# A gate as a VectorE dot product, W loaded by two queues, and w2 ahead of a shuffle

## Chip, cores and metric

One core of a Trainium2 chip. The metric is device time in microseconds (us) of one execution; medians are given with the range of all runs. Ratios are the mean time of one kernel's fast runs over that of the other's of the same rounds, with a 95% interval, so they are not quite the ratio of the medians quoted. The kernel before runs 144.71 us (144.64 to 145.56, three runs).

## The reference, cut to what matters

```python
x = A_x                                        # 2048 x 512 (and a batch of 1)
g = sigmoid((x * gate_w).sum(-1, keepdims=True))
a = irfft2(rfft2(x) * (w_r + 1j * w_i))        # spectral branch, W is 2048 x 257
h = x @ w1 + b1                                # dense branch, 512 -> 1792
b = (h * tanh(softplus(h))) @ w2               # 1792 -> 512
return g * a + (1 - g) * b
```

## The kernel before

Everything is in bf16 with float32 sums. The spectral branch is written as small DFT matmuls. It runs in stages: column transforms (s1) and row transforms (A1) of 16 row blocks, a shuffle through scratch in DRAM (four writes, four reads), the middle stage (s2, the products with W on VectorE, s2i), a second shuffle, and two inverse stages (s1i, a1i). The dense branch has 56 groups of four matmuls in layer 1 and 34 groups of seven in layer 2. Its groups fill TensorE wherever the spectral branch has nothing ready.

The order on each engine is fixed when the kernel is built. A scheduler in the kernel's own source lists the tasks by priority with planned durations; a transfer is planned at a bandwidth written beside it. The engines then run these lists in order and wait on semaphores.

```python
DMA_BW = 370e3          # planned bytes per us of a transfer
W_BW = 150e3            # the same, for the reversed rows of W
...
            if t.isdma:                                   # in schedule()
                xs = max(est + t.dur + 1.2, bw_free)
                bw_free = xs + t.xfer                     # one transfer after the other
                t.done = bw_free + 0.9
...
        def wload(nm, dst, src_t, o):                     # W: plain and reversed half
            v = src_t.rearrange("(g h e2 j) k -> g h e2 j k", g=16, h=2, e2=2)
            dma(f"ld_{nm}p", dst[0:32, :, :].rearrange("p j k -> p (j k)"), v[:, 0, ...]...,
                32 * 16448, writes=[(o, 0)])
            nb = dst[32:64, :, :]
            ...
            dma(f"ld_{nm}r", back(0, 31, 16, 32, 2), n1, 16 * 32 * 514, writes=[(o, 1)], bw=W_BW)
            dma(f"ld_{nm}n", back(1, 31, 16, 31, 2), n0, 16 * 31 * 514, writes=[(o, 2)], bw=W_BW)
            ...
        wload("wr", Wa, A_w_r, "Wa")
        wload("wi", Wb, A_w_i, "Wb")
        dma("ld_sm", SM[:], d_c["SM"][:], ...)            # matrices of the middle stage
        # W's upper partitions: four copies on VectorE, with a high priority
                G.add(f"cp{o}{h}", [("dve", ..., lambda e, ...: e.tensor_scalar(
                    out=W[64:128, js, :], in0=W[0:64, js, :], scalar1=sc, ...))],
                      reads=[(o, i) for i in range(4)], writes=[(o, 4, h)], prio=PR["cp"])
...
        for h in range(2):                                # w2 waits for the shuffle's writes
            dma(f"ld_w2_{h}", w2_sb[:, 7 * h:7 * (h + 1), :], ..., writes=[("w2", h)],
                deps=t_r1w, queue="pool")
        # the shuffle's reads overwrite x_sb; t_r1w are its writes
            t_r1r.append(dma(f"r1r{h}", In2[:, 8 * h:8 * h + 8, :]..., reads=[("scr1", i) for i in range(4)], ...))
...
        def f_gate(e):                                    # gate: 64 one-column matmuls
            for t in range(NT):
                for dt_ in range(4):
                    ins = e.matmul(ps[:, bk(sl_g), t:t + 1], xT[:, dt_, t, :], gw_sb[:, dt_:dt_ + 1], ...)
```

## Time and profile before

| | before |
|---|---|
| time, median | 144.71 us |
| last A1 matmul starts | 30.61 us |
| last write of the first shuffle landed, reads issued | 37.97 us |
| first s2 matmul | 42.0 us, after a wait of 0.8 |
| granted TensorE clock | 1.00 |

How to read it: TensorE is nearly always busy, so the time is its work plus its holes. The lines of the profile itself stand in the prediction.

### The profile page before, as it was taken

To read this page: it belongs to the slowest core of one execution; us is meant where nothing else is said; L and a number is where in the kernel's file an instruction comes from. 1 tells how busy PE (TensorE), PEld (TensorE's weight loads), DVE (VectorE), ACT (ScalarE), POOL (GpSimd) and SP (SyncE) were. 2 spreads that over 40 slices of the span, in tenths; PEclk is the share of its full clock that TensorE was granted. 3 is DMA by queue.
4 is the path that set the end of the run, shared out by engine and by line. 5 is a ranking of instruction groups with operands and counts; after the bars stand their busy time and mean duration, and the time that the engine had idled before them with its cause. 6 is when DMAs were issued, how large, how long until landed. Compare 5 with 4: busy or idle time off the path is not lost.

```text
span 142.7 us, 2376 instructions
## 1 busy us (share of the span) xinstructions
PE 134.9 (95%) x866; PEld 72.9 (51%) x881; DVE 86.1 (60%) x188; ACT 82.9 (58%) x139; POOL 3.9 (3%) x10
## 2 busy tenths in 40 slices
PE   6999999778979999999999999999999999999992
PEld 2476665554434444434444465455456565555471
DVE  2448694974009999999971031002999985899331
ACT  3289888776867877779984573855154344431000
POOL 1000000000160000000000000000000000000000
PEclk9999999999999999999999999999999999999999
DMA  4999999999299999580303695000012120100121
GB/s 117 302 405 408 249 172 151 150 307 336 74 310 359 364 317 145 131 283 0 147 0 152 174 292 121 0 0 5 0 74 76 74 76 5 74 0 36 43 108 39
DMA packets 20463, 21.66 MB, mean 152 GB/s; under 512 B 5156, under 2 KB 16932, under 8 KB 20388
## 3 DMA queue, kind: packets, MB, share of 16 engines
q1 hardware_dynamic: 19712, 18.89, 49.6%
q0 software_dynamic: 704, 2.62, 5.2%
q8 instruction: 7, 0.11, 0.3%
q14 instruction: 4, 0.03, 0.1%
q10 hardware_dynamic: 36, 0.00, 0.0%
HBM read 14.17 MB, written 6.29 MB: 143 GB/s over the span
## 4 chain that ended last, share of the span: by engine, by line
PE 70%; DVE 13%; DMA 7%; ACT 4%; issue 3%; DVEq 0%; SPq 0%
PE ps L824 28%; PE ps L804 21%; PE ps L885 5%; PE ps L530 4%; DMA scr<-R 4%; DVE PX L764 3%; DVE PX L760 3%; DVE PX L763 3%; DMA R<-scr 3%; PE ps L866 3%; PE ps L654 2%; ACT R L516 2%; DVE PX L767 2%; DVE R L515 1%; PE ps L779 1%
## 5 line engine op out<-in xcount | busy, mean ns | idle before, releaser
L824 PE MATMUL ps<-w_sb,hsb 128*128 128x512 bf16 (+1 forms) x232 | 51.3, 366 | 0.6 <-DMA w_sb<-in_B_w_dram 0.2
L804 PE MATMUL ps<-xT,w_sb 128*128 128x512 bf16 x215 | 51.3, 379 | 0.4
L812 ACT ACTIVATE hsb<-ps,b1f 128x512 bf16<-128x512 f32 x56 | 37.7, 689 | 11.1 <-PE ps L804 10.8
L516 ACT ACTIVATE R<-ps 128x512 bf16<-128x512 f32 (+1 forms) x43 | 24.7, 596 | 16.3 <-PE ps L824 11.2
L824 PEld LDWEIGHTS ps<-w_sb,hsb 128*128 128x128 bf16 x238 | 22.7, 98 | 22.4 <-DMA w_sb<-in_B_w_dram 0.5
L804 PEld LDWEIGHTS ps<-xT,w_sb 128*128 128x128 bf16 x224 | 21.2, 98 | 22.9 <-ACT xT L621 0.2
L516 ACT ACTIVATE PX<-ps 128x512 bf16<-128x512 f32 (+1 forms) x19 | 10.5, 551 | 6.8 <-PE ps L885 4.2
L515 DVE CAST R<-ps 128x512 bf16<-128x512 f32 (+1 forms) x17 | 11.3, 689 | 3.3 <-PE ps L654 1.6
L876 ACT ACTIVATE TT<-ps 128x512 bf16<-128x512 f32 x11 | 6.4, 595 | 6.5 <-PE ps L866 6.4
L897 DVE SCALAR_TENSOR_TENSOR PX<-ps,gcol,R 128x512 f32<-128x512 f32 x12 | 9.0, 751 | 1.4 <-DVE R L891 0.5
L873 DVE CAST TT<-ps 128x512 bf16<-128x512 f32 x5 | 3.4, 689 | 9.7 <-PE ps L866 8.9
L885 PE MATMUL ps<-GD,TT 128*128 128x256 bf16 x64 | 9.0, 273 | 0.0
L530 PE MATMUL ps<-GD 128*128 128x512 bf16 x18 | 7.3, 522 | 1.3 <-DVE GD L527 1.3
L885 PEld LDWEIGHTS ps<-GD,TT 128*128 128x128 bf16 x64 | 6.2, 98 | 3.3 <-DVE TT L873 0.3
L852 DVE TENSOR_SCALAR gcol<-gth 128x16 f32<-128x16 f32 x1 | 0.2, 174 | 12.3 <-ACT gth L849 12.3
L767 DVE TENSOR_TENSOR PX<-PX 128x512 bf16<-128x512 bf16 x16 | 6.8, 425 | 1.0
L763 DVE TENSOR_TENSOR PX<-PX,Wb 64x512 bf16<-64x512 bf16 x16 | 6.8, 422 | 0.5
L764 DVE TENSOR_TENSOR PX<-PX,Wb 64x512 bf16<-64x512 bf16 x16 | 6.7, 421 | 0.2
L760 DVE TENSOR_TENSOR PX<-PX,Wa 128x512 bf16<-128x512 bf16 x16 | 6.7, 421 | 0.1
L923 DVE SCALAR_TENSOR_TENSOR R<-ps,omg,R 128x512 bf16<-128x512 f32 (+1 forms) x5 | 3.2, 643 | 5.8 <-PE ps L824 5.8
L903 DVE SCALAR_TENSOR_TENSOR R<-ps,gcol,PX 128x256 bf16<-128x256 f32 x12 | 5.8, 484 | 0.4
L654 PEld LDWEIGHTS ps<-CF,R 128*128 128x128 bf16 x64 | 4.7, 101 | 2.6 <-issue 0.6
(93 smaller groups left out, 110.9 us busy)
## 6 DMA issues: line engine op xcount, KB each, us to landing
scr<-R SPq DMA_DIRECT2D x8, 512.0 KB, 4.6
R<-scr SPq DMA_DIRECT2D x8, 512.0 KB, 6.0
w_sb<-in_B_w_dram SPq DMA_DIRECT2D x2, 896.0 KB, 8.8
w_sb<-in_B_w_dram POOLq DMA_DIRECT2D x2, 896.0 KB, 11.4
out_dram<-R SPq DMA_DIRECT2D x7, 256.0 KB, 2.0
R<-in_A_x_dram SPq DMA_DIRECT2D x3, 512.0 KB, 11.3
SM<-c_sm SPq DMA_DIRECT2D x1, 576.0 KB, 10.9
Wa<-in_A_w_r_dram SPq DMA_DIRECT2D x1, 514.0 KB, 13.9
```

The costliest lines, as they stand in the source:

```text
L515: G.add(name, [("dve", dve_dur(n), lambda e: e.tensor_copy(out=outf(), in_=inf())), ("act", act_dur(n), lambda e: e.activation(outf(), inf ...
L516: ("act", act_dur(n), lambda e: e.activation(outf(), inf(), AF.Copy))],
L530: G.add(f"warm{i}", [("pe", 0.43 if i < 7 else 0.22, lambda e, sl=sl: e.matmul(ps[:, bk(sl), :], GDf[:, 0:128], GDf[:, 0:512], start=True, ...
L760: return e.tensor_tensor(out=v(P1, sP, 0, 128), in0=v(Xb, sX, 0, 128), in1=Wa[:, js, 0:256], op=ALU.mult)
L763: e.tensor_tensor(out=v(P2, sQ, 0, 64), in0=v(Xb, sX, 64, 128), in1=Wb[64:128, js, 0:256], op=ALU.mult)
L764: return e.tensor_tensor(out=v(P2, sQ, 64, 128), in0=v(Xb, sX, 0, 64), in1=Wb[0:64, js, 0:256], op=ALU.mult)
L767: return e.tensor_tensor(out=P1[:, sP.i, :], in0=P1[:, sP.i, :], in1=P2[:, sQ.i, :], op=ALU.add)
L804: ins = e.matmul(ps[:, bk(sl), :], w1_sb[:, dt_, 128 * ft:128 * (ft + 1)], xT[:, dt_, 4 * c:4 * c + 4, :], start=(dt_ == 0), stop=(dt_ == 3))
L812: return e.activation(hsb[:, hb, ft, :], ps[:, bk(sl), :], AF.Mish, bias=b1f[:, ft:ft + 1])
L824: ins = e.matmul(ps[:, bk(sl), 0:n1 - n0], hsb[:, hb, ft, 128 * tl:128 * (tl + 1)], w2_sb[:, ft, n0:n1], start=(ft == 0), stop=(ft == NFT ...
L885: ins = e.matmul(ps[:, bk(sy), 256 * hh:256 * (hh + 1)], TT[:, st.i, i, :], GD[:, i, :], start=(i % 2 == 0), stop=(i % 2 == 1))
L897: return e.scalar_tensor_tensor(out=o, in0=ps[:, bk(sy), 0:256].unsqueeze(1).to_broadcast([128, 2, 256]), scalar=gcol[:, t:t + 1], in1=ya[ ...
```

## The change

The intent is fourfold. The gate leaves TensorE: VectorE multiplies and sums x with gate_w in an idle stretch. The W copies go behind the last evacuation of the front, so that A1 waits less. W's reversed rows come by GpSimd's queue while the plain rows come by SP's. w2 is loaded ahead of the shuffle, so that layer 2 can start early. The planned bandwidths are changed with it. The diff, cut to its core (left out: reordered loads of x and w1 with planned bandwidths of their own, the smaller transpose without gate_w, planned durations of the warming matmuls, and a priority):

```diff
-DMA_BW = 370e3
+DMA_BW = 380e3
-W_BW = 150e3
+W_BW = 260e3
...
             dma(f"ld_{nm}p", dst[0:32, :, :]..., 
-                32 * 16448, writes=[(o, 0)])
+                32 * 16448, writes=[(o, 0)], bw=260e3)
...
-            dma(f"ld_{nm}r", back(0, 31, 16, 32, 2), n1, 16 * 32 * 514, writes=[(o, 1)], bw=W_BW)
+            dma(f"ld_{nm}r", back(0, 31, 16, 32, 2), n1, 16 * 32 * 514, writes=[(o, 1)], bw=W_BW, deps=t_wq, queue="pool")
   (the same for the other reversed rows)
...
         dma("ld_sm", SM[:], d_c["SM"][:], 128 * 2 * 128 * len(MATS), writes=["SM"])
-        (the four W copies stood here)
+        for h in range(2):
+            dma(f"ld_w2_{h}", w2_sb[:, 7 * h:7 * (h + 1), :], ..., 128 * 7 * 1024,
+                writes=[("w2", h)])
...
-        for h in range(2):
-            dma(f"ld_w2_{h}", ..., writes=[("w2", h)], deps=t_r1w, queue="pool")
...
+                G.add(f"cp{o}{h}", ..., reads=[(o, i) for i in range(4)], writes=[(o, 4, h)], deps=t_e2, prio=PR["cp"])
...
+            t_gx.append(G.add(f"gx{t}", [("dve", 0.8, lambda e, t=t: e.scalar_tensor_tensor(
+                out=gscr[:, t % 3, :], in0=x_sb[:, t, :], scalar=1.0, in1=gwb[:, :], op0=ALU.mult, op1=ALU.mult, accum_out=gacc[:, t:t + 1]))],
+                reads=[("x", t), "gwb"], writes=[("gacc", t), ("gscr", t % 3)], deps=t_e2, prio=PR["cp"] + 0.2))
...
-                reads=[("scr1", i) for i in range(4)], writes=[("In2", h)], deps=t_x1, prio=PR["ld"] + 1))
+                reads=[("scr1", i) for i in range(4)], writes=[("In2", h)], deps=t_x1 + t_gx[4 * h:4 * h + 4], prio=PR["ld"] + 1))
...
-        (f_gate and its 64 matmuls)
+        G.add("gth", [("act", 1.6, lambda e: e.activation(gth[:, :], gacc[:, :], AF.Tanh, scale=0.5))],
+              reads=[("gacc", t) for t in range(NT)], writes=["gth"], deps=t_hs, prio=PR["gate"])
```

More of the change, by code (lines that the diff above doesn't have):

```diff
@@ L433, in _build @@
         tz = sb("tz", [128, 2, 32], F32)
-        bgraw = sb("bgraw", [18, 128], BF)
+        bgraw = sb("bgraw", [NFT, 128], BF)
         b1f = sb("b1f", [128, NFT], F32)
-        gw_sb = sb("gw_sb", [128, 4], BF)
+        gwb = sb("gwb", [128, 512], BF)
+        gacc = sb("gacc", [128, NT], F32)
         gth = sb("gth", [128, NT], F32)
@@ L455, in _build @@
         ya = R4[:].rearrange("p (t d) -> p t d", t=NT)
+        gscr = TT[:].rearrange("p i a b -> p i (a b)")
         MI = {n: SM[:, i, :] for i, n in enumerate(MATS)}
@@ L514, in evac @@
         def evac(name, outf, inf, n, reads, writes, prio, bias=0.0):
-            G.add(name, [("dve", dve_dur(n), lambda e: e.tensor_copy(out=outf(), in_=inf())),
+            t = G.add(name, [("dve", dve_dur(n), lambda e: e.tensor_copy(out=outf(), in_=inf())),
                          ("act", act_dur(n), lambda e: e.activation(outf(), inf(), AF.Copy))],
-                  reads=reads, writes=writes, prio=prio).bias = bias
+                  reads=reads, writes=writes, prio=prio)
+            t.bias = bias
+            return t
         G.add("ones", [("pool", 0.2, lambda e: e.memset(ident[:, :], 1.0))], writes=["ones"], prio=100)
@@ L529, in _build, with ld_x @@
         for i in range(NWARM):
-            G.add(f"warm{i}", [("pe", 0.43 if i < 7 else 0.22, lambda e, sl=sl: e.matmul(ps[:, bk(sl), :], GDf[:, 0:128], GDf[:, 0:512], start=True, stop=True))],
+            G.add(f"warm{i}", [("pe", 0.42 if i < 5 else 0.22, lambda e, sl=sl: e.matmul(ps[:, bk(sl), :], GDf[:, 0:128], GDf[:, 0:512], start=True, stop=True))],
                   reads=["GD"], writes=[sl], slots=[sl] if i == 0 else (), prio=-100.0)
         t_x = []
-        def ld_x(a, b, queue="sp"):
-            t_x.append(dma(f"ld_x{a}", x_sb[:, a:b, :], xv[:, a:b, :], 128 * 1024 * (b - a), writes=[("x", i) for i in range(a, b)], queue=queue))
+        def ld_x(a, b, bw=DMA_BW):
+            t_x.append(dma(f"ld_x{a}", x_sb[:, a:b, :], xv[:, a:b, :], 128 * 1024 * (b - a), writes=[("x", i) for i in range(a, b)], bw=bw))
         dma("ld_b1", bgraw[0:14, :], B_b1.rearrange("(ft p) -> ft p", p=128), 3584, writes=["braw"], queue="act", prio=200.0)
-        dma("ld_gw", bgraw[14:18, :], gate_w.rearrange("(dt p) -> dt p", p=128), 1024, writes=["gwraw"], queue="act", prio=200.0)
         def ld_c(i, c0, c1, writes):
@@ L545, in ld_w1 @@
             f = slice(896 * h, 896 * h + 896)
-            dma(f"ld_w1_{h}", w1_sb[:, :, f], w1v[:, :, f], 128 * 4 * 1792, writes=[("w1", h)])
-        ld_x(0, 1)
-        ld_c(0, 0, 1280, ["FD", ("FT", 0)])
-        ld_x(1, 4)
+            dma(f"ld_w1_{h}", w1_sb[:, :, f], w1v[:, :, f], 128 * 4 * 1792, writes=[("w1", h)], bw=380e3 if h else 340e3)
+        ld_x(0, 1, bw=600e3)
+        ld_c(0, 0, 1792, ["FD", ("FT", 0)])
+        ld_x(1, 4, bw=270e3)
+        ld_x(4, 8, bw=300e3)
         ld_w1(0)
-        ld_c(1, 1280, 2816, [("FT", 1)])
-        ld_x(4, 8)
+        ld_c(1, 1792, 2816, [("FT", 1)])
         ld_w1(1)
@@ L556, in _build @@
         ld_x(12, 16)
+        dma("ld_gw", gwb[:], bass.AP(gate_w.tensor, gate_w.offset, [[0, 128], [1, 512]]), 128 * 1024, writes=["gwb"])
         def wload(nm, dst, src_t, o):
@@ L569, in wload @@
             n1 = bass.AP(src_t.tensor, src_t.offset + 65 * 257, [[128 * 257, 16], [257, 32], [1, 257]])
-            dma(f"ld_{nm}r", back(0, 31, 16, 32, 2), n1, 16 * 32 * 514, writes=[(o, 1)], bw=W_BW)
+            dma(f"ld_{nm}r", back(0, 31, 16, 32, 2), n1, 16 * 32 * 514, writes=[(o, 1)], bw=W_BW, deps=t_wq, queue="pool")
             n0 = bass.AP(src_t.tensor, src_t.offset + 97 * 257, [[128 * 257, 16], [257, 31], [1, 257]])
-            dma(f"ld_{nm}n", back(1, 31, 16, 31, 2), n0, 16 * 31 * 514, writes=[(o, 2)], bw=W_BW)
+            dma(f"ld_{nm}n", back(1, 31, 16, 31, 2), n0, 16 * 31 * 514, writes=[(o, 2)], bw=W_BW, deps=t_wq, queue="pool")
             s64 = bass.AP(src_t.tensor, src_t.offset + 64 * 257, [[128 * 257, 16], [1, 257]])
-            dma(f"ld_{nm}s", nb[1:32:2, 0, :], s64, 16 * 514, writes=[(o, 3)], bw=W_BW)
+            dma(f"ld_{nm}s", nb[1:32:2, 0, :], s64, 16 * 514, writes=[(o, 3)], bw=W_BW, deps=t_wq, queue="pool")
+        t_wq = t_x[-2:-1]
         wload("wr", Wa, A_w_r, "Wa")
@@ L578, in _build @@
         dma("ld_sm", SM[:], d_c["SM"][:], 128 * 2 * 128 * len(MATS), writes=["SM"])
-        for o, W in (("Wa", Wa), ("Wb", Wb)):
-            for h in range(2):
-                js = slice(16 * h, 16 * h + 16)
-                sc = 1.0 if o == "Wa" else -1.0
-                G.add(f"cp{o}{h}", [("dve", dve_dur(4112, 4), lambda e, W=W, js=js, sc=sc: e.tensor_scalar(
-                    out=W[64:128, js, :], in0=W[0:64, js, :], scalar1=sc, scalar2=None, op0=ALU.mult))],
-                      reads=[(o, i) for i in range(4)], writes=[(o, 4, h)], prio=PR["cp"])
+        for h in range(2):
+            dma(f"ld_w2_{h}", w2_sb[:, 7 * h:7 * (h + 1), :], w2v[:, 7 * h:7 * (h + 1), :], 128 * 7 * 1024,
+                writes=[("w2", h)])
         WA = [("Wa", i) for i in range(4)] + [("Wa", 4, h) for h in range(2)]
@@ L590, in _build @@
         sl = fslot()
-        def f_tr_small(e, sl=sl):
-            return e.transpose(psb[:, bk(sl), 0:18], bgraw[0:18, :], ident[0:18, 0:18])
-        G.add("tr_small", [("pe", 0.1, f_tr_small)], reads=["braw", "gwraw", "ident"], writes=[sl], slots=[sl], prio=PR["mid"])
-        def f_ev_small(e, sl=sl):
-            e.tensor_copy(out=b1f[:, :], in_=psb[:, bk(sl), 0:14])
-            return e.tensor_copy(out=gw_sb[:, :], in_=psb[:, bk(sl), 14:18])
-        G.add("ev_small", [("dve", 0.25, f_ev_small)], reads=[sl], writes=["b1f", "gw"], prio=PR["tr"])
-        wl = []
+        G.add("tr_small", [("pe", 0.1, lambda e, sl=sl: e.transpose(psb[:, bk(sl), 0:NFT], bgraw[:, :], ident[0:NFT, 0:NFT]))],
+              reads=["braw", "ident"], writes=[sl], slots=[sl], prio=PR["mid"])
+        G.add("ev_small", [("dve", 0.15, lambda e, sl=sl: e.tensor_copy(out=b1f[:, :], in_=psb[:, bk(sl), 0:NFT]))],
+              reads=[sl], writes=["b1f"], prio=PR["tr"])
         def tr(t):
@@ L623, in tr @@
             G.add(f"evx{t}", [("dve", 0.43, f_evx), ("act", 0.6, f_evx_a)], reads=[sl], writes=[("xT", t)], prio=PR["tr"] + 0.2 if t < 4 else 90.2).bias = BIAS
-        t_x1, t_a1, t_s1, t_r1w = [], [], [], []
+        t_x1, t_a1, t_s1, t_e2, t_r1w = [], [], [], [], []
         for t in range(NT):
@@ L655, in f_s1 @@
                     return ins
-                t_s1.append(G.add(f"s1_{t}_{half}", [("pe", pe_dur(128, 2), f_s1)], reads=[("XB", i, to) for i in keys] + [("FT", min(t // 4, 1))],
+                t_s1.append(G.add(f"s1_{t}_{half}", [("pe", pe_dur(128, 2), f_s1)], reads=[("XB", i, to) for i in keys] + [("FT", t // 8)],
                                   writes=[sl], slots=[sl] if half else (), prio=PR["s1"]))
@@ L672, in _build @@
                               writes=[sl], slots=[sl], prio=PR["a1"]))
-            evac(f"e2_{t}", lambda t=t: A1s[:, t, :].rearrange("p (c q m) -> p c q m", c=2, m=4),
-                 lambda sl=sl: ps[:, bk(sl), :].rearrange("p (c m q) -> p c q m", c=2, m=4), 512, [sl], [("A1s", t)], PR["a1"] + 0.2, BIAS)
+            t_e2.append(evac(f"e2_{t}", lambda t=t: A1s[:, t, :].rearrange("p (c q m) -> p c q m", c=2, m=4),
+                 lambda sl=sl: ps[:, bk(sl), :].rearrange("p (c m q) -> p c q m", c=2, m=4), 512, [sl], [("A1s", t)], PR["a1"] + 0.2, BIAS))
             if t % 4 == 3:
@@ L679, in _build @@
                                  reads=[("A1s", i) for i in range(a, a + 4)], writes=[("scr1", t // 4)], prio=PR["ld"] + 1))
-        for h in range(2):
-            dma(f"ld_w2_{h}", w2_sb[:, 7 * h:7 * (h + 1), :], w2v[:, 7 * h:7 * (h + 1), :], 128 * 7 * 1024,
-                writes=[("w2", h)], deps=t_r1w, queue="pool")
         dma("ld_gd", GD[:], d_c["GD"][:], 128 * 2048, writes=["GD"], deps=t_r1w, queue="pool")
         dma("ld_gt", GT, d_c["GT"][:], 128 * 4096, writes=["GT"], deps=t_s1 + t_r1w, queue="pool")
+        for o, W in (("Wa", Wa), ("Wb", Wb)):
+            for h in range(2):
+                js = slice(16 * h, 16 * h + 16)
+                sc = 1.0 if o == "Wa" else -1.0
+                G.add(f"cp{o}{h}", [("dve", dve_dur(4112, 4), lambda e, W=W, js=js, sc=sc: e.tensor_scalar(
+                    out=W[64:128, js, :], in0=W[0:64, js, :], scalar1=sc, scalar2=None, op0=ALU.mult))],
+                      reads=[(o, i) for i in range(4)], writes=[(o, 4, h)], deps=t_e2, prio=PR["cp"])
+        t_gx = []
+        for t in range(NT):
+            t_gx.append(G.add(f"gx{t}", [("dve", 0.8, lambda e, t=t: e.scalar_tensor_tensor(
+                out=gscr[:, t % 3, :], in0=x_sb[:, t, :], scalar=1.0, in1=gwb[:, :], op0=ALU.mult, op1=ALU.mult, accum_out=gacc[:, t:t + 1]))],
+                reads=[("x", t), "gwb"], writes=[("gacc", t), ("gscr", t % 3)], deps=t_e2, prio=PR["cp"] + 0.2))
         t_r1r = []
@@ L710, in _build @@
         G.add("tabe", [("dve", 0.25, lambda e: e.tensor_copy(out=tz[:, :, :], in_=ps[:, bk(sl_t), 0:64].rearrange("p (a j) -> p a j", a=2)))],
-              reads=[sl_t], writes=["tz"], prio=PR["mid"])
+              reads=[sl_t], writes=["tz"], prio=PR["mid"] + 0.6)
         sl_z = fslot()
@@ L836, in _build @@
                     G.tasks[-1].deps.extend(t_r1w)
-        sl_g = mslot()
-        def f_gate(e):
-            ins = None
-            for t in range(NT):
-                for dt_ in range(4):
-                    ins = e.matmul(ps[:, bk(sl_g), t:t + 1], xT[:, dt_, t, :], gw_sb[:, dt_:dt_ + 1], start=(dt_ == 0), stop=(dt_ == 3))
-            return ins
-        G.add("gate", [("pe", 64 * 0.03, f_gate)], reads=[("xT", t) for t in range(NT)] + ["gw"], writes=[sl_g], slots=[sl_g], deps=t_hs[-2:-1], prio=PR["gate"])
-        G.add("gth", [("act", 1.6, lambda e: e.activation(gth[:, :], ps[:, bk(sl_g), 0:NT], AF.Tanh, scale=0.5))],
-              reads=[sl_g], writes=["gth"], deps=t_hs, prio=PR["gate"])
+        G.add("gth", [("act", 1.6, lambda e: e.activation(gth[:, :], gacc[:, :], AF.Tanh, scale=0.5))],
+              reads=[("gacc", t) for t in range(NT)], writes=["gth"], deps=t_hs, prio=PR["gate"])
         for nm, o, sc in (("gcol", gcol, 0.5), ("omg", omg, -0.5)):
```

## The prediction

> **What bounds the kernel now.** I read the page first (busy times, then the chain that ended last), then the waits of the matmul engine, the chain in order of time, the timeline of VectorE in the front, and the windows table for the transfers.
>
> ```profile
> span 142.7 us, 2376 instructions
> PE 134.9 (95%) x866; PEld 72.9 (51%) x881; DVE 86.1 (60%) x188; ACT 82.9 (58%) x139; POOL 3.9 (3%) x10
> PE 70%; DVE 13%; DMA 7%; ACT 4%; issue 3%; DVEq 0%; SPq 0%
> ```
>
> TensorE is busy 95% of the span, and 70% of the last chain is on it. The matmul start runs at 1.26 us and the last matmul ends at 140.1; behind it lie one VectorE output operation and a store, 2.6 us. So the time is TensorE's work in its fixed order, plus the holes in it. The holes that are named:
>
> ```profile
> PE ps L666 <- DVE R L515: 1.5, 2, 0.8
> PE ps L748 <- DMA R<-scr: 0.8, 1, 0.8
> PE ps L703 <- ACT hsb L812: 0.5, 1, 0.5
> ```
>
> L666 is the row transform of the spectral branch (stage "A1"), L748 the first matmul behind the first shuffle (through scratch in DRAM), L703 the small table of W's edge columns. In the chain in order of time:
>
> ```profile
> 31.93 5.95 DMA scr<-R
> 37.97 4.03 DMA R<-scr
> 62.98 1.73 PE ps L804 x8
> 95.81 1.58 PE ps L845 x64
> 129.50 10.62 PE ps L824 x63
> 140.15 0.48 DVE R L923
> ```
>
> Eight dense 512-column matmuls take 1.73 us, 216 ns each. The gate's 64 one-column matmuls (L845) hold TensorE for 1.58 us. The last 10.6 us are dense layer 2 alone: the spectral branch is done before, so its lateness costs nothing unless it makes TensorE wait. What made the two L666 waits is on VectorE:
>
> ```profile
> 25.09 1.23 DVE L583 TENSOR_SCALAR Wa<-Wa 64x4112 bf16<-64x4112 bf16 x1 [1.94 <-DMA Wa<-in_A_w_r_dram]
> 26.34 1.29 DVE L515 CAST R<-ps 128x512 bf16<-128x512 f32 x2
> 27.66 1.23 DVE L583 TENSOR_SCALAR Wa<-Wa 64x4112 bf16<-64x4112 bf16 x1
> 28.92 1.29 DVE L515 CAST R<-ps 128x512 bf16<-128x512 f32 x2
> 42.48 0.69 DVE L515 CAST PX<-ps 128x512 bf16<-128x512 f32 x1 [7.86 <-PE ps L749]
> ```
>
> A W copy of 1.23 us stands ahead of each pair of evacuations that A1 waits for; and VectorE idles 7.9 us during the first shuffle. The transfers:
>
> ```profile
> 12.00:16.00 4.00, 3.89 (x39) 2.38 (x38) 2.79 (x7) 3.35 (x8) 0.00 (x0) 1.00 1.15 385
> 16.00:20.00 4.00, 3.95 (x37) 2.57 (x34) 3.96 (x8) 3.87 (x7) 0.00 (x0) 1.00 1.07 149
> 24.00:28.00 4.00, 3.23 (x28) 2.01 (x26) 2.85 (x4) 3.05 (x6) 0.00 (x0) 1.00 1.19 142
> ```
>
> The last two columns are the DMA engines' busy share and GB/s. While W loads (16 to 29 us) the engines are as busy as before, at 145 GB/s in place of 385: its reversed rows are 514-byte packets. In the ten microseconds from 16 us there were 1814 packets, nearly all of these; 16 engines x 10 us x 1.1 busy, less about 30 for the large packets, gives some 81 ns for each.
>
> **What the Trainium skill says.** "TensorE: Matmul & The Clock Gate", section "Wait — 56ns, not 53.3ns?", gives 215.7 ns from start to start for a warm 512-column matmul; the 216 ns above agree, so dense matmuls cannot get cheaper and only holes and removed work count. "DMA: Bandwidth & Descriptors", section "Queues, rings and completion order", says an engine takes turns between queues packet by packet, and section "Issuing engines are not separate DMA queues" that several issuers end on the same 16 engines and save only issue time. If that holds, a second queue hides little of the 81 ns; the trace before shows no small-packet load beside another queue, so it is open. "VectorE: DVE Perf Modes", section "Two Vector instructions with no wait between them", says that an operation which also writes its accumulator is two instructions; no such operation is in the trace before.
>
> **The change part by part.**
>
> *Gate.* Off TensorE: 1.58 us. On VectorE come 16 multiply-and-accumulate operations of 128x512. The same operation from PSUM takes 751 ns (L897 row); from SBUF it should be a little shorter, plus the accumulator's second instruction: I take 0.75, together 12.0 us. They wait for every A1 evacuation and come before the second half of the shuffle, since their input x is what the shuffle's reads overwrite: the four reads each need four of them.
>
> *W copies.* Four of 1.23 us leave the front, 4.9 us of VectorE, and now follow the gate products, among the first multiplications of the middle stage.
>
> *Front.* By the order of instructions, TensorE has the same 18 warming matmuls and one dense group (four matmuls, 0.865) fewer ahead of the last A1: 10 in place of 11. A1 ended at 30.67. Less 0.87 for the group, less 1.5 for the two waits, gives 28.3. The second block of x is now loaded ahead of dense weights, so all transposes and the first eight column transforms come early; going through the first 14 us with the durations of the trace I find about 0.5 us more work done. A1 ends at about 28.0, and the last evacuation at 29.0 in place of 31.8.
>
> *TensorE after A1.* 46 groups of dense layer 1 x 0.865 = 39.8; 32 half groups of layer 2 x 1.512 = 48.4; 32 middle matmuls x 0.216 = 6.9; small ones 0.8; inverse stages 3.6 + 7.0. Sum 106.5. Before, the like sum was 107.2 (one layer-1 group fewer, gate 1.58 more), and 140.1 - 30.7 = 109.4 were taken, so 2.2 us were holes: 1.2 named above (L748, L703), 1.0 small ones. The table matmuls now stand far behind in the order and the first shuffle read has 16 dense groups (13.8 us) ahead of its first user, in place of 11, so the 1.2 should go. The 1.0 stays.
>
> *Middle stage, the new tightness.* VectorE: start 29.0, gate 12.0 -> 41.0; W copies 4.9, 64 multiplications x 0.425 = 27.2, nine evacuations x 0.65 = 5.9, small ones 1.0: 39.0, at the 95% busy of that stage before, 41. End 82. The second shuffle then took 3.0 for the write and 5 to the first use: about 90. TensorE reaches the first inverse matmul after 39.8 + 13.6 (nine half groups of layer 2) + 7.7 + 1.0 from 28.0: also 90. Before there was much room here (the middle ended at 75), now none: I put 1.0 us of new waits on it.
>
> *Transfers.* From x's end at about 15 us the SP queue has 0.13 (gate row) + 1.05 (W plain) + 0.59 + 1.83 MB (w2), then 2.1 MB of shuffle: 5.7 MB, 15 us at 385 GB/s. The reversed W rows, 2048 x 81 ns / 16 = 10.4 us of engine time, come beside it. Half hidden, the shuffle's write ends near 35.5 and its first read near 39.5, ahead of TensorE's 41.8. w2 is there long before layer 2 wants it.
>
> *Sum.* 28.0 + 106.5 + 1.0 + 1.0 = 136.5; tail 2.6: span 139.1. Time less span was 144.7 - 142.7 = 2.0 (1.7 in the profiled run), say 1.9: **141.0 us**, 2.6% less.
>
> **The rivals.** (1) *VectorE becomes the bound of the middle.* For it: 17 us of new work on the stretch, no room. Against: 8 us of it fall into an idle hole, and layer 2 has work to fill with. If one product takes 0.85, or VectorE waits more often, the inverse starts 2 us later: 143. (2) *The shuffle queues behind w2 and W.* For it: the skill's one-set-of-engines sentence. With nothing hidden the reversed rows push the write to 41 and the first read to 45, a hole of 3 to 4 us: 144 to 145. Against: small packets that cost 81 ns where bytes alone would cost 23 look like latency, which a second queue could fill. (3) *The front gains nothing*, because ScalarE (3.4 of 4 us busy there) paces it: then only the gate and the 1.2 go, 142.5. (4) *All goes well*, the middle holds step: 139.5.
>
> **Range and chances.** Everything known is a gain of 4 to 5 us, everything feared takes 1 to 4 back. The line of 2% is 141.8. I take 139.5 to 143.8; faster 0.60, same 0.33, slower 0.07.
>
> **What would show it.** Right: no L845-like matmuls; the two A1 waits gone and the last A1 near 28; VectorE busy through 29 to 41 with gate products of about 750 ns; the wait for the first shuffle read absent; the last A1 evacuation near 29; the first inverse matmul near 90. Wrong: a wait of TensorE for the first shuffle read over 1 us (transfers), waits for multiplications on VectorE in 45 to 90 us summing to over 2 us (VectorE), an A1 that ends after 29.5 (front). A time over 143.8 would mean that the transfers did not overlap at all.

## The result, and the profile after

The changed kernel runs **149.23 us** (148.3 to 151.12, four runs) against 144.68 (144.51 to 145.56, four runs) of the kernel before in the same rounds: ratio 1.028, interval 1.0207 to 1.0354. It is slower, and outside the predicted range.

The page of the kernel after, its span, busy times and the chain that ended last by engine:

```profile
span 147.8 us, 2277 instructions
PE 135.4 (92%) x803; PEld 71.6 (48%) x817; DVE 98.7 (67%) x224; ACT 80.4 (54%) x134; POOL 5.6 (4%) x14
PE 76%; DVE 11%; DMA 7%; ACT 3%; issue 1%; DVEq 0%; SPq 0%
```

TensorE is busy 135.4 us, no less than the 134.9 of before, although the gate is gone from it: 134.9 less the gate's 1.58 is 133.3, so the same matmuls took 2.1 us longer. And TensorE is idle 12.4 us of the span, where it was idle 7.8. The waits of TensorE (what it waited for: us in total, times, longest):

```profile
PE ps L754 <- DMA R<-scr: 6.8, 1, 6.8
PE ps L534 <- DVE GD L531: 1.3, 1, 1.3
```

L754 is the first s2 matmul; it waits 6.8 us for the shuffle's read, in place of 0.8. The other wait is the start and was there before. The chain in order of time (start, length, what):

```profile
29.95 8.12 DVE TT L689 x27
...
39.42 5.84 DMA scr<-R
...
45.34 4.20 DMA R<-scr
49.59 0.40 PE ps L754
...
51.48 3.30 PE ps L810 x8
...
134.61 10.62 PE ps L830 x63
```

The gate products (L689) begin at 29.95. The shuffle's last write ends at 45.3 in place of 37.9, its read at 49.5, and eight dense matmuls (L810) then take 3.30 us in place of 1.73. The chain leads from the gate products to the shuffle's last write. That link is inferred from semaphores, and no write depends on a gate product in the program; before_w2_early below has the write just as late (45.3) without any gate on VectorE. In the windows table (length; busy time of PE, PEld, DVE, ACT, POOL; granted clock, DMA share, GB/s) one sees both the cause and that second loss:

```profile
16.00:20.00 4.00, 3.58 (x31) 2.64 (x33) 3.09 (x5) 3.96 (x8) 3.58 (x6) 1.00 1.02 195
20.00:24.00 4.00, 4.00 (x38) 2.50 (x36) 3.88 (x9) 3.20 (x7) 0.18 (x1) 1.00 0.92 176
24.00:28.00 4.00, 3.95 (x41) 2.93 (x40) 2.24 (x4) 3.31 (x7) 0.00 (x0) 1.00 1.03 160
...
48.00:52.00 4.00, 2.19 (x6) 1.05 (x8) 1.31 (x2) 0.60 (x1) 0.00 (x0) 0.50 1.02 395
52.00:56.00 4.00, 4.00 (x14) 1.59 (x13) 3.73 (x5) 1.37 (x2) 0.00 (x0) 0.68 0.62 247
```

From 16 to 28 us the DMA engines move 195, 176 and 160 GB/s, where the kernel before moved 149, 178 and 142 with W on one queue. The queues apart, first in 18 to 22 us, where only SP's queue (q1) moves anything large, then in 24 to 32 us with GpSimd's (q0) beside it (packets, MB, share of the 16 engines' time):

```profile
q1 hardware_dynamic: 109, 0.75, 94.4%
q0 software_dynamic: 299, 0.89, 67.9%
q1 hardware_dynamic: 300, 0.44, 35.6%
```

So W's plain rows, with the first packets of SM among them, move at only some 190 GB/s though no reversed packet runs beside them, and the engines are 94% busy. GpSimd issues the reversed rows from 16.4 us on, but in the packet records their first packet starts at 23.5, just before the last plain one (24.1): the two halves of W hardly ran side by side.

After the hole the clock is at 0.50 and 0.68 of full speed. "TensorE: Matmul & The Clock Gate", section "What's actually happening", says that TensorE falls to half its clock after an idle window of some 3.4 us and needs as long a busy one to come back. These windows agree in kind: 0.96 in 44 to 48 us and 0.68 in 52 to 56 put the half clock at about 47.7 to 54.5, from 4.9 us into the hole to 4.9 us after its end. The extra busy time of TensorE is this: the same matmuls, slower. The issues on SP's queue show who stood ahead of the shuffle (start, how long issuing took, what):

```profile
9.27 0.58 SPq L492 DMA_DIRECT2D SM<-c_sm  x1
9.90 8.72 SPq L492 DMA_DIRECT2D w_sb<-in_B_w_dram  x2
18.79 21.90 SPq L492 DMA_DIRECT2D scr<-R  x4
```

SM was issued at 9.27 and landed 22.1 us later, at 31.4; w2, issued right behind it, landed at about 38 to 39. The four writes took SP 21.9 us to issue, the first alone 12.4.

Last, the groups of the page (line, engine, operation, out and in, count; busy time and mean ns of one; idle ahead):

```profile
L689 DVE SCALAR_TENSOR_TENSOR TT<-R,gwb 128x512 bf16<-128x512 bf16 x16 | 9.9, 688 | 0.2 <-DVE R L517 0.2
```

16 gate products hold VectorE for 9.9 us; each is 688 ns with an 83 ns accumulator read that overlaps the next.

**How the plan differs from the chip.** The kernel's scheduler can be asked what it planned. These are dates of its list, not measurements:

| | planned | on the chip |
|---|---|---|
| before: shuffle's last write ends | 33.8 | 37.9 |
| after: SM landed | 22.7 | 31.4 |
| after: w2 landed | 25.2, 27.6 | about 38, 39 |
| after: shuffle's last write ends | 37.1 | 45.3 |
| after: first read landed | 41.2 | 49.5 |

The list puts 16 dense groups ahead of the first s2, which is right for 41.2 and 8 us too few for 49.5.

### The profile page after: what moved, and what is told of

Read it like the earlier page. It is cut to its first block, busy times and chain, and to the rows that moved or that the text cites. A ratio compares the mean times of both kernels' runs of the same rounds, so it can differ in the third digit from the quotient of the medians.

```text
span 147.8 us, 2277 instructions
## 1 busy us (share of the span) xinstructions
PE 135.4 (92%) x803; PEld 71.6 (48%) x817; DVE 98.7 (67%) x224; ACT 80.4 (54%) x134; POOL 5.6 (4%) x14
## 3 DMA queue, kind: packets, MB, share of 16 engines
q0 software_dynamic: 608, 1.84, 5.6%
## 4 chain that ended last, share of the span: by engine, by line
PE 76%; DVE 11%; DMA 7%; ACT 3%; issue 1%; DVEq 0%; SPq 0%
PE ps L830 33%; PE ps L810 20%; DVE TT L689 6%; PE ps L881 5%; PE ps L534 4%; DMA scr<-R 4%; DMA R<-scr 3%; PE ps L862 2%; PE ps L648 2%; PE ps L756 2%; PE ps L785 2%; PE ps L606 1%; DVE R L517 1%; PE ps L660 1%; PE ps L661 1%
## 5 line engine op out<-in xcount | busy, mean ns | idle before, releaser
L810 PE MATMUL ps<-xT,w_sb 128*128 128x512 bf16 x217 | 52.8, 388 | 0.4
L830 PE MATMUL ps<-w_sb,hsb 128*128 128x512 bf16 (+1 forms) x232 | 51.7, 366 | 0.3
L810 PEld LDWEIGHTS ps<-xT,w_sb 128*128 128x128 bf16 x224 | 21.9, 100 | 25.0 <-issue 1.9
L830 PEld LDWEIGHTS ps<-w_sb,hsb 128*128 128x128 bf16 x238 | 22.7, 98 | 21.1
L518 ACT ACTIVATE R<-ps 128x512 bf16<-128x512 f32 (+1 forms) x38 | 21.6, 597 | 18.7 <-PE ps L830 15.5
L517 DVE CAST R<-ps 128x512 bf16<-128x512 f32 (+1 forms) x22 | 14.6, 687 | 6.1 <-PE ps L648 2.2
L518 ACT ACTIVATE PX<-ps 128x512 bf16<-128x512 f32 (+1 forms) x18 | 9.9, 561 | 14.1 <-PE ps L755 6.7
L869 DVE CAST TT<-ps 128x512 bf16<-128x512 f32 x4 | 2.8, 691 | 11.4 <-PE ps L862 11.4
L872 ACT ACTIVATE TT<-ps 128x512 bf16<-128x512 f32 x12 | 6.9, 594 | 6.0 <-PE ps L862 5.7
L689 DVE SCALAR_TENSOR_TENSOR TT<-R,gwb 128x512 bf16<-128x512 bf16 x16 | 9.9, 688 | 0.2 <-DVE R L517 0.2
L517 DVE CAST PX<-ps 128x512 bf16<-128x512 f32 x1 | 0.7, 691 | 9.6 <-PE ps L755 9.6
L754 PE MATMUL ps<-R,SM 128*128 128x256 bf16 x1 | 0.4, 396 | 6.8 <-DMA R<-scr 6.8
## 6 DMA issues: line engine op xcount, KB each, us to landing
SM<-c_sm SPq DMA_DIRECT2D x1, 576.0 KB, 22.1
```

Of the source, the lines that this page charges most:

```text
L517: t = G.add(name, [("dve", dve_dur(n), lambda e: e.tensor_copy(out=outf(), in_=inf())), ("act", act_dur(n), lambda e: e.activation(outf(), ...
L518: ("act", act_dur(n), lambda e: e.activation(outf(), inf(), AF.Copy))],
L689: t_gx.append(G.add(f"gx{t}", [("dve", 0.8, lambda e, t=t: e.scalar_tensor_tensor(out=gscr[:, t % 3, :], in0=x_sb[:, t, :], scalar=1.0, in ...
L810: ins = e.matmul(ps[:, bk(sl), :], w1_sb[:, dt_, 128 * ft:128 * (ft + 1)], xT[:, dt_, 4 * c:4 * c + 4, :], start=(dt_ == 0), stop=(dt_ == 3))
L830: ins = e.matmul(ps[:, bk(sl), 0:n1 - n0], hsb[:, hb, ft, 128 * tl:128 * (tl + 1)], w2_sb[:, ft, n0:n1], start=(ft == 0), stop=(ft == NFT ...
L872: return e.activation(TT[:, st.i, :, :].rearrange("p a b -> p (a b)"), ps[:, bk(sk), :], AF.Copy)
```

## The experiments

**Theory.** Moving w2 and W to where they now stand makes the shuffle late, because all transfers share the same DMA engines and W's rows don't go faster on two queues. The order on TensorE was laid out for transfers that are faster than they are. The hole of 6.8 us and the low clock after it eat the gain. **Rivals:** the gate products make VectorE the bound, or hold back the shuffle; the software queue for the reversed rows is what slows the transfers; the early w2 is a mistake in itself, whatever the order.

Every run gave correct results. "Orders kept" means that the scheduler ran as in the parent kernel and its lists were edited afterwards, so nothing else moves. "Replanned" means that the scheduler was free. In the first batch the kernel before ran 144.77 us (143.81 to 148.01, seven runs), in the second 144.43 (143.71 to 146.22, nine runs), in the third 145.31 (144.43 to 145.83, seven runs). Each batch ran on a chip of its own, so ratios of different batches are compared with care.

### w2_late_frozen: only w2 goes back, orders kept

```diff
         order = G.schedule()
+        for h in range(2):                     # to GpSimd's queue, behind the shuffle's writes
+            w = by[f"ld_w2_{h}"]
+            order["sp"].remove(w)
+            order["pool"].insert(order["pool"].index(by["ld_gd"]), w)
+            w.deps.extend(t_r1w)
```

> The kernel after, with every engine's instruction order kept; only the two w2 loads leave the SP queue and go to the Pool queue behind the shuffle's writes, where the kernel before had them. Theory (w2 ahead on the SP queue delays the shuffle): the writes end 5 us earlier or more (1.83 MB at 350 GB/s), near 38 to 40 instead of 45.3; TensorE's 6.8 us wait for the first shuffle read falls below 2 us and the clock stays full; a new wait of 1 to 3 us for w2 may appear, since layer 2 stands early in this order. 141 to 144 us. Rival (the small W rows alone delay the shuffle, w2 only rides along): the writes still end after 43 and the time stays above 147.

146.77 us (145.19 to 148.59), ratio 1.0049 (0.9949 to 1.0148), unclear: two runs were at 145.2 and 145.4 with a clock of 1.00 and 0.99, two at 148 with a mean clock of 0.977, which count as slow. 141 to 144 was expected. The profile is of one of the slow runs. The shuffle's writes end at 39.7 in place of 45.3. The waits of TensorE:

```profile
PE ps L830 <- DMA w_sb<-in_B_w_dram: 3.7, 1, 3.7
PE ps L754 <- DMA R<-scr: 1.8, 1, 1.8
```

So moving w2 back makes the shuffle 5.6 us earlier, and the wait for its read falls from 6.8 to 1.8. But layer 2 (L830), which the order calls for early, now waits 3.7 us for w2: one hole for another.

### w2_late_replanned: only w2 goes back, scheduler free

```diff
-        for h in range(2):
-            dma(f"ld_w2_{h}", ..., writes=[("w2", h)])
...
+        for h in range(2):
+            dma(f"ld_w2_{h}", ..., writes=[("w2", h)], deps=t_r1w, queue="pool")
```

> As the run before, but the kernel's own scheduler may reorder for the late w2, so layer 2 does not stand where w2 has not come. Theory: 140 to 143 us, without a wait of TensorE over 1.5 us behind 30 us. Rival (gate and W copies on VectorE cost the middle stage more than the front gains): 144 us or more, with the waits for VectorE between 50 and 95 us.

147.78 us (147.27 to 148.61), ratio 1.0226 (1.0149 to 1.0303). The writes end at 40.9, 4.4 us earlier than after, yet TensorE waits 7.2 us for the first read: freed of w2, the scheduler believed the shuffle to be still earlier and put 43 matmuls of layer 1 ahead of it in place of 64. This is the first sign that the order counts, and not the date of the transfer alone.

### fill_hole: 29 useless matmuls ahead of the first s2, orders kept

```diff
+            for _ in range(29):
+                ins = e.matmul(ps[:, bk(sx), :], w1_sb[:, 0, 0:128], w1_sb[:, 0, 0:512], start=True, stop=True)
...
+        order["pe"].insert(order["pe"].index(by["s2_0"]), fill)
```

> The kernel after, plus 29 matmuls of no use (6.3 us) put ahead of the first middle matmul, where TensorE otherwise waits 6.8 us. The wait as such stays, so if the lower clock behind the wait (the trace after shows 0.50 in 48 to 52 us and 0.68 in 52 to 56) costs time of its own, the kernel gets 1.5 to 2.5 us faster: about 147. If the clock costs nothing on the path: 149.2 unchanged.

147.04 us (146.56 to 147.19), ratio 1.0164 (1.01 to 1.0227). The clock is 1.00 in all four runs, and the wait for the read falls to 1.5 us because TensorE is busy with nothing useful. The stall is as long as before, only the clock is kept: 149.23 - 147.04 gives **2.2 us for the lower clock** (the two ratios, 1.028 - 1.0164 times 144.7, give 1.7). The rest of the loss is the hole itself, less what the other parts of the change gain.

### before_w2_early: only w2 moves ahead of the shuffle, in the kernel before

```diff
+        for h in (1, 0):
+            w = by[f"ld_w2_{h}"]
+            order["pool"].remove(w)
+            order["sp"].insert(order["sp"].index(by["ld_sm"]) + 1, w)
+            w.deps = []
```

> The kernel before, instruction orders kept, with only its two w2 loads moved from the Pool queue to the SP queue ahead of the shuffle's writes. Theory: the first shuffle read lands 4 to 6 us later than its 42 us, TensorE waits 4 to 6 us there, and the time rises to 148 to 151 us (wait plus lower clock, less what an earlier w2 gives). Rival (bandwidth to spare ahead of the shuffle): within 1 us of 144.7.

151.51 us (150.57 to 153.36), ratio 1.0457 (1.0369 to 1.0546). The profile is of the slowest run, which counts as slow. TensorE waits 3.0 us in A1, and 6.0 us for the first read (reads issued at 45.3):

```profile
PE ps L748 <- DMA R<-scr: 6.0, 1, 6.0
```

So moving w2 under a fixed order costs more than the whole change. No gate on VectorE, no second queue is needed for the hole.

### one_queue: W's reversed rows back on SP's queue, orders kept

```diff
+        for nm in ("wr", "wi"):
+            at = order["sp"].index(by[f"ld_{nm}p"])
+            for k in "snr":
+                w = by[f"ld_{nm}{k}"]
+                order["pool"].remove(w)
+                order["sp"].insert(at + 1, w)
+                w.deps = []
```

> The kernel after, all orders kept, but W's reversed halves go back to the SP queue behind the plain ones (w2 stays ahead of the shuffle). If the second queue hides nothing, because all of W is written into partitions 0 to 63 (the Trainium skill, SBUF page, gives 189 to 196 GB/s for such a target at 1 MiB, and the trace after shows 165 to 190 GB/s with one queue or two): the shuffle's writes end at 44 to 46 us as in the kernel after, or 1 to 2 us earlier because the Pool queue's late start is gone; 147 to 150 us. If the second queue does help: they end after 48 and the time is 152 or more.

148.77 us (148.12 to 149.57), ratio 1.0341 (1.0282 to 1.04): no different from the change. The writes end at 43.65, 1.7 us *earlier* than with two queues, and the wait is 5.5 us. From 16 to 28 us the engines moved 173, 177 and 154 GB/s, against 195, 176 and 160. As it is used here, the second queue hides nothing.

### ports_split: the reversed rows to other partitions, orders kept otherwise

"SBUF — State Buffer", section "Door 1: The DMA port swizzle (why `[64,N]` ≈ `[32,N]`)", says that partitions 0 to 31 and 0 to 63 reach the same 8 of 16 ports, with 189 and 196 GB/s measured for 1 MiB. W's plain rows go to partitions 0 to 31 and the reversed ones to 32 to 63. Here the reversed rows go to 96 to 127, which by that page use the other eight, and four more copies on VectorE bring them where they are used.

```diff
-            nb = dst[32:64, :, :]
+            nb = dst[96:128, :, :]
...
+                G.add(f"cq{o}{h}", [("dve", ..., lambda e, W=W, js=js: e.tensor_scalar(
+                    out=W[32:64, js, :], in0=W[96:128, js, :], scalar1=1.0, ...))], ..., deps=t_e2, prio=PR["cp"])
```

> The kernel after, with the reversed halves loaded into partitions 96 to 127 (plain: 0 to 31) and copied back by four more VectorE copies of 1.23 us; results stay right. If only the ports of partitions 0 to 63 are the limit and two queues on different ports run side by side: W and SM are in near 27 us in place of 33.5, the shuffle's writes end near 38 and TensorE's wait of 6.8 us falls below 1.5 us; 141 to 144 us. If, as the skill's page says of two transfers on the two halves, they still take turns on the same engines (6% more only): writes end at 44 to 46, time 148 to 152, the more copies included.

148.59 us (147.52 to 150.5), ratio 1.037 (1.0271 to 1.0469): no different from the change. The writes end at 44.4 in place of 45.3. The queues in 24 to 32 us, to be held against those of the kernel after:

```profile
q0 software_dynamic: 330, 0.88, 66.7%
q1 hardware_dynamic: 389, 0.48, 38.2%
```

That is 170 GB/s in place of 166. But the run does not test what it was meant to test: the first reversed packet starts at 23.2 us and the last plain one at 23.3, so the halves hardly ran side by side here either. (From 16 to 20 us this kernel moved 216 GB/s in place of 195, but with no reversed packet in it.) It shows only that the reversed rows go no faster to the other partitions. The plain rows go to partitions 0 to 31 as before, and their 190 GB/s agrees with the page's 189. The same page, section "Can I just issue two DMAs to hit both halves?", says 6% for a pair on two halves, and that they take turns; no run here shows it.

### replan_w2_early: two planned bandwidths, nothing else

```diff
-W_BW = 260e3
+W_BW = 120e3
...
-                32 * 16448, writes=[(o, 0)], bw=260e3)
+                32 * 16448, writes=[(o, 0)], bw=150e3)
```

> The kernel after with two numbers of its scheduler's transfer model changed (W rows 260 to 120 GB/s, plain half 260 to 150), so that its plan has the shuffle's writes end where the chip has them (44.8 in the plan, 45.3 measured; the kernel after planned 37.1). The transfers are the same; only the order on the engines differs, with layer 2 of the dense branch ahead of the first middle matmul. If the loss is an order laid out for a shuffle that comes 8 us later than planned: no wait of TensorE over 1.5 us, the writes still at 44 to 46, time 140.5 to 143. If the late shuffle costs time whatever TensorE does meanwhile (the spectral branch then ends last): 146 or more, with new waits near the first inverse matmul.

**140.85 us** (140.21 to 141.05), ratio 0.978 (0.9746 to 0.9814). This is the changed kernel with two numbers that no engine ever sees, only the scheduler. They are fitted and not measured rates: with them the planned end of the last write, 44.8, falls near the traced 45.3 (the plain rows moved at some 190 GB/s and are planned at 150). It is the fastest kernel of the study, 2.2% under the kernel before. Its page:

```profile
span 139.0 us, 2305 instructions
PE 134.1 (96%) x817; PEld 71.0 (51%) x817; DVE 97.5 (70%) x222; ACT 81.9 (59%) x136; POOL 5.6 (4%) x14
```

Its chain in order of time, where the hole was:

```profile
29.11 15.54 PE ps L810 x72
44.65 4.53 PE ps L830 x21
...
49.49 1.53 PE ps L830 x7
```

And the window in which TensorE had stood idle:

```profile
44.00:48.00 4.00, 4.00 (x20) 1.82 (x19) 0.64 (x1) 1.49 (x3) 0.91 (x2) 1.00 0.31 66
```

The writes end at 45.84, no earlier than after (45.34). The transfers are as slow as they were. But now 72 matmuls of layer 1 and 28 of layer 2 stand between A1 and the first s2, in place of 64 of layer 1, and the wait for the read is gone from the list; the clock is 1.00 in all runs. This settles the cause: not the late shuffle, but the lateness that the order did not know of. VectorE's middle stage, with the gate products ahead of it, makes TensorE wait 0.3 us, so the rival of a VectorE bound falls.

### replan_w2_late: corrected bandwidths, but w2 behind the shuffle as before

```diff
-W_BW = 260e3
+W_BW = 110e3
   (plain rows 150e3, and w2 as in w2_late_replanned)
```

> The same correction of the plan (W rows 110, plain 150 GB/s) with w2 behind the shuffle on the Pool queue, where TensorE has only layer 1 to do while it waits: 142 to 145. It tells what w2 ahead is worth once the plan is right: if w2 ahead pays, this is 1 to 3 us slower than the run before it.

149.29 us (146.31 to 149.75; three of the four runs count as slow, with a mean clock of 0.977, so no ratio is given; 142 to 145 was expected). The profile is of the fast one, 146.31. The writes end at 37.8, the earliest of all, and TensorE waits elsewhere:

```profile
PE ps L830 <- DMA w_sb<-in_B_w_dram: 3.4, 1, 3.4
```

With a corrected plan for W and w2 late, TensorE waits for w2 itself. So the early w2 is no mistake in itself: under a corrected plan it is the part that fills the hole, here a median of 140.85 against the one fast run of 146.31.

### before_replan_w2_early: w2 early and corrected bandwidths in the kernel before

```diff
-W_BW = 150e3
+W_BW = 100e3
...
-                32 * 16448, writes=[(o, 0)])
+                32 * 16448, writes=[(o, 0)], bw=150e3)
...
+        for h in range(2):
+            dma(f"ld_w2_{h}", ..., writes=[("w2", h)])     # behind SM, on SP's queue
```

> The kernel before with only w2 moved ahead of the shuffle's writes on the SP queue and its plan corrected (W 100 and 150 GB/s), no gate on VectorE, no copies moved, no second queue. If the right plan with an early w2 is the whole gain of the best kernel so far (140.9): 141 to 142. If gate and copies pay their 3 us (1.6 + 1.5) beside it: 143 to 145.

144.02 us (143.8 to 144.31), ratio 0.9926 (0.9878 to 0.9974), clock 1.00. The same w2 that cost 4.6% under the old order gains 0.7% under one that knows of it.

### best_one_queue: the fastest kernel with W on one queue

```diff
 (replan_w2_early, and:)
-            dma(f"ld_{nm}r", ..., bw=W_BW, deps=t_wq, queue="pool")
+            dma(f"ld_{nm}r", ..., bw=W_BW)                 # W_BW 125e3; the others alike
```

> The best kernel so far with W's reversed halves back on the SP queue and the plan set to match (W rows 125 GB/s). If the second queue gives nothing: 140.5 to 142. If it gives something once the plan is right: 142.5 or more.

142.6 us (141.77 to 143.0), ratio 0.9817 (0.9767 to 0.9867), against 0.978 for two queues in the batch before. The intervals overlap, and they do not rule out a difference of one per cent either way. The two ran on different chips and have orders of their own, so this stays open.

### best_gate_on_tensor: the fastest kernel with the gate back on TensorE

```diff
 (replan_w2_early, and:)
-            t_gx.append(G.add(f"gx{t}", ...scalar_tensor_tensor...))
...
+                    ins = e.matmul(ps[:, bk(sl_g), t:t + 1], xT[:, dt_, t, :], gw_sb[:, dt_:dt_ + 1], ...)
```

> The best kernel so far with the gate's dot product back as 64 one-column matmuls on TensorE and the 9.9 us of products off VectorE. TensorE is the bound, so 1.6 us slower: 142 to 143. If instead VectorE's products cost the middle stage anything, the difference is smaller: 140.5 to 141.5.

143.95 us (143.51 to 144.57), ratio 0.992 (0.987 to 0.997), against 0.978. The move of the gate is worth 1.4 points, some 2.0 us; its matmuls took 1.58. The two ratios are of different chips and orders; against best_one_queue of the same batch (0.9817) it is 1.0 point. What is left without it, 0.992, is what the kernel before reaches too with an early w2 and corrected bandwidths (0.9926). So no gain of the other parts (copies, load order, second queue) is visible beside these two.

### before_copies_behind: only the W copies move, in the kernel before, orders kept

```diff
+        cps = [t for t in order["dve"] if t.name.startswith("cpW")]
+        for t in cps:
+            order["dve"].remove(t)
+        at = max(i for i, t in enumerate(order["dve"]) if t.name.startswith("e2_")) + 1
+        order["dve"][at:at] = cps
+        order["pe"].remove(by["tab"])                      # the table of W's edge columns
+        order["pe"].insert(order["pe"].index(by["s2_0"]), by["tab"])
```

> The kernel before, orders kept, with only the four W copies moved behind the last front evacuation on VectorE (and the small table matmuls behind the dense groups, so that they do not wait for the copies). A1's two waits of 1.5 us go in any case. If the front is what counts: 143 to 143.5. If the shuffle's writes are held by the transfers (W and SM land at 31 to 32, then 2.1 MB at 340 GB/s), they still end near 38, TensorE waits 1.5 us more for the first read and the time stays at 144 to 145.

147.0 us (144.63 to 147.2); three of four runs count as slow (mean clock 0.977), so no ratio. The profile is of the fast one, at 144.63 with a clock of 0.988. The last A1 matmul starts at 28.78 in place of 30.61: the copies did cost the front 1.8 us. The timeline of TensorE where that went:

```profile
38.65 0.16 PE L706 MATMUL ps<-Wb,SM 128*128 128x1 bf16 x1
41.50 0.40 PE L748 MATMUL ps<-R,SM 128*128 128x256 bf16 x1 [2.69 <-DMA R<-scr]
```

The first s2 comes at 41.5, where it came at 42.0. The shuffle ends when W's loads let it, not when A1 is done, so 1.8 us of front turn into a wait of 2.69 in place of 0.8. And the clock is 0.62 in the four microseconds from 40 to 44 us. The span, 142.9, is that of the kernel before (142.7). **A faster front is worth nothing while the transfers are not faster and the order has nothing to put in.**

## Why the prediction was wrong, point by point

**What failed: the step "Transfers".** It has the shuffle's write end "near 35.5 and its first read near 39.5, ahead of TensorE's 41.8", from 5.7 MB at 385 GB/s with the reversed rows "half hidden". The chip had 45.3 and 49.5. From x's end at 15 us to SM's landing at 31.4 about 16 us went by, where that step allows 1.77 MB at 385 GB/s, 4.6 us, and half of 10.4, which is 9.8 together. The mistake has two parts. Plain W was put at 385 GB/s, a rate of transfers to 128 partitions, though it goes to 32; the SBUF page's 189 GB/s for such a load was not looked up. By the packet records its 64 packets took 83.6 us together, 5.2 us of the 16 engines, where 1.05 MB at 385 GB/s is 2.7. And the small packets were taken for latency that a second queue would fill. one_queue shows that it fills none; GpSimd's packets, most of them 4112 bytes and 385 ns, took 6.2 us of the engines in full.

Two readings led there. The 145 GB/s "while W loads" leaves out a window with 178; from 16 to 29 us it was 158. And the 81 ns of a small packet were 70 in the records, because the large packets in those ten microseconds took 60 us and not the 30 allowed for them: the plain rows were the slow part that was overlooked.

**What was missed besides.** The step ends at the first read; the prediction took a hole of that size for its own length only. The clock after it cost some 2 us more (fill_hole). Rival 2, "The shuffle queues behind w2 and W", is what happened. It expected the write at 41, the read at 45 and a hole of 3 to 4 us; each came 4 us later, and the clock came on top. 149.2 less 6.8 for the hole less the 2.1 of longer matmuls is 140.3, near the 141.0 of the sum.

**And the step behind that.** "The first shuffle read has 16 dense groups ahead of its first user" was read as a margin. It is a margin only if the plan that set it to 16 is true. That plan used 260 GB/s for W, and the trace of the kernel before (158 GB/s from 16 to 29 us) already said otherwise; the prediction quoted that stretch and the 16 groups and did not set them side by side.

**What held.** The gate's 1.58 us: the move is worth some 1.5 to 2.0 (1.0 and 1.4 points, best_gate_on_tensor). The gate products: 9.9 us in place of 12.0, as predicted in kind. *Front*: the two A1 waits of 0.8 went (0.6 is left), and the last A1 started 1.84 us earlier, ending at 29.0 where 28.0 was predicted; the last evacuation ended at about 29.7, predicted 29.0. *TensorE after A1* and the tail: in replan_w2_early, where the hole and the clock are taken away, the sum of 141.0 meets 140.85. Its first inverse matmul starts at 94.5, not 90, but layer 2 fills the time and no wait appears. So the sum is right for TensorE's work and in part by luck in its dates, and the order is not the one it was reckoned for. Rival 1 (VectorE) had no part: 0.3 us of waits for its products. Rival 3 (no gain in front) is refuted by the dates of A1. Even so, before_copies_behind shows that the front's gain alone does not reach the end.

**What stays open.** Whether the second queue is worth its 0.4 points in the fastest kernel. Why the same hole costs 1.2% of mean clock in one run of a kernel and 2.3% in the next, with 2 to 3 us of time (before_copies_behind, w2_late_frozen). The traces' clock records show half-clock stretches of 3.41 us (before_copies_behind) or 6.83 us (after, w2_late_frozen), which is 1.2 or 2.3% of these spans. So a run that counts as slow here may be one that had the longer stretch; why it comes is not shown. And what sets W's rate of 150 to 200 GB/s: not the second queue; the ports are untested, and the plain rows' rate agrees with them.

## What to carry to other kernels

Where an order is laid out at build time, compare its planned dates with the traced ones before judging any change of transfers: two corrected bandwidths turned a loss of 2.8% into a gain of 2.2%. Transfers that are brought forward push back all behind them on the same engines; ask which wait ends there, and whether the engine has other work placed ahead of it. A hole on TensorE can cost more than its length (some 2 us more for the 6.8 here), so reckon the clock after it.

## What the Trainium skill lacked or had wrong

- "DMA: Bandwidth & Descriptors", section "Issuing engines are not separate DMA queues", says that issuing on several engines saves only issue time, which is usually small against the transfer. The runs agree on the transfers (writes end at 45.3 with two queues, 43.7 with one). But issue time is not small behind a long backlog: the first shuffle write took SP 12.4 us to issue, and four took 21.9. That section does not say so.
- "SBUF — State Buffer", section "Door 1: The DMA port swizzle (why `[64,N]` ≈ `[32,N]`)": its 189 GB/s for 32 partitions fits the plain rows here (190 from 18 to 22 us, with some of SM). Nothing in it is shown wrong.
- "TensorE: Matmul & The Clock Gate", section "What's actually happening", gives about 3.4 us of idling for the fall of the clock. In before_copies_behind the clock record has it fall at 40.9 us, within a wait of 2.69 us that eight narrow matmuls precede; dense work ended at about 38.3, 2.6 us before the fall. The section does not tell how little work counts as idle.
